# Value products joined in pairs, lower weight halves from PE, 14 raw buffers, and a refitted order

## The chip, the cores and the metric

The kernel runs on one core of one Trainium2 chip. Its engines are PE (matrix products, results in PSUM), DVE (vectors), ACT (activations and copies), POOL (general elementwise work in SBUF) and SP, whose queue issues all transfers. The metric is the device time of one launch in microseconds. PE's clock has two levels, 1.2 and 2.4 GHz; the profile shows the level that was granted as 0.50 or 1.00, and means between them.

## What is computed

Attention that keeps the 32 largest scores of each row, then a gated layer, then a layer with a softmax weighting and a normalization. The weights come as float64 words.

```python
def _attn_ref(q, k, v):            # batch 4, heads 8, rows 576, width 64
    scores = scale * np.matmul(q, k.transpose(0, 1, 3, 2))
    kth = np.partition(scores, -top_k, axis=-1)[..., -top_k:-top_k + 1]      # top_k = 32
    scores = np.where(scores >= kth, scores, -1000000000.0)
    attn = np.exp(scores - np.max(scores, axis=-1, keepdims=True))
    return np.matmul(attn / (np.sum(attn, axis=-1, keepdims=True) + 1e-09), v)

def _moe_ref(x, w_gate, w_val, w_out):          # 2304 x 512, hidden 1536
    gate = 1.0 / (1.0 + np.exp(-(x @ w_gate)))
    return gate * (x @ w_val) @ w_out

def _moe2_ref(x, w_in, w_out, g_ln):            # hidden 1024
    h = x @ w_in
    e = np.exp(h - np.max(h, axis=-1, keepdims=True))
    solu = h * e / (np.sum(e, axis=-1, keepdims=True) + 1e-09)
    ln = (solu - mean(solu)) / np.sqrt(var(solu) + 1e-06) * g_ln
    return ln @ w_out
```

## The kernel before

**Tiles.** The 2,304 rows are cut into 18 chunks of 128. A chunk has four attention steps of two heads each, 72 steps in all. In a step PE makes the scores (`scores`, L645), ACT takes them out of PSUM, DVE folds them (L656, L660) and finds the 32 largest in four rounds (L670, L674), ACT masks and exponentiates, and ACT and POOL split the result into two float16 halves (L732, L736). The queue on SP transposes both halves into a tile `et` (`flip_halves`, L743; two buffers), and PE multiplies them with the values (`attend`, L758): 30 matmuls of 64 columns of weights and 128 moving columns, two column halves of the array side by side. At the last step of a chunk PE spreads the inverse sums over the columns (`spread`, L723, also 64 columns wide), ACT copies them out (L785), and DVE scales the rows by them (L788). Then come the layers of the chunk, all products of float16 halves in three terms: gate and value (`group`, L894), down (L940), hidden (L977), last (L1088).

**Weights.** Five weights are read in 52 pieces of 128 x 512 words: gate 12, value 12, down 12, input 8, output 8, in this order. The first 36 pieces land in eight raw buffers that lie in the space of the last two weights, piece n behind piece n-8; the others land in `big`. DVE rebuilds float32 words from the two halves of each raw word (`rebuild`): two operations for the pieces in `ADDED` (the first 24), whose low bits ACT converts (`rest`, L443) and POOL adds (`add_rest`, L447); three operations for the others, the third being `low` (L433). When a weight's norm is known, a scale is formed and each piece is split: ACT writes a scaled float32 copy (`split_hi`, L501) and a float16 upper half (`split_first`, L505), and POOL subtracts (`split_lo`, L508).

**What sets the order.** Every operation is handed to a planner (`Order.add`) with an engine, a cost, a rank, its needs and the buffers that it takes and frees. The planner plays the five queues through (`play`), with a lag from each engine to each other (`SEEN`), and writes the instructions out in the order found. `SHIFT` moves ranks by kind of operation. On the chip every engine runs its instructions in that order. The first products of each weight wait for all its pieces: `done[...]` is the list of the last operations of the pieces.

Of the kernel before, what the change touches and what calls it, by code (L numbers as in the profile page):

```python
# [56 lines left out]
ADDED = tuple(range(24))  # L57
SCALED = ()
STAGED = 36
SHIFT = {  # L60
# [68 lines left out]
}  # L129
WKEYS = ("g", "v", "o1", "i", "o2")  # L130
LAYERS = ("sg", "ga", "va", "gt", "gi", "gl", "vf", "hi", "la", "th", "tl", "tf", "tu")
LONE = ("lh", "ll", "lr", "do", "n2", "p2", "s2", "mh", "mf", "ml", "l0", "l1", "l2", "l3", "ld", "l4", "fi", "sd")

# [1105 lines left out]
```

## Time and profile before

| | |
|---|---|
| median of three runs | 992.6 us (990.73 to 993.14) |
| profiled execution, its own time | 992.24 us |
| its span | 990.5 us |
| PE busy | 872.0 us (88%) |
| DVE busy | 841.0 us (85%) |
| ACT busy | 750.4 us (76%) |
| POOL busy | 617.4 us (62%) |
| 16 DMA engines, mean busy share | 45.2% on the queue of the transfers |

Busy time is the time in which an engine has an instruction under way; matmuls overlap, and their ends are modelled. In a timeline the distance between the starts of two neighbours tells what the first one cost PE, while the length printed for it contains the overlap. A row of a group of instructions gives the line, the engine, the operation, target and source, the count, then the total busy time, the mean of one in ns, and the idle time ahead of them. The span has three parts: a front in which the weights are rebuilt and the first attention steps run, a long middle, and the layers of the last chunks.

### The profile page before, as it was taken

The page shows a single profiled execution, that of the slowest core. Times are in us where ns is not written, and L with a number is a line of the kernel's source. Part 1 is how long each engine was busy: PE and PEld are TensorE (multiplying, and loading weights), DVE is VectorE, ACT ScalarE, POOL GpSimd, SP SyncE. Part 2 cuts the span into 40 slices and gives each one's busy share as a digit, 9 for nine tenths or more (in the row PEclk, how much of TensorE's full clock was granted, in tenths as well). Part 3 has the DMA queues.
Part 4 walks back from the last instruction along what each step waited for, and adds up shares of the span by engine and source line. Part 5 has one row for each costly group of instructions (what it writes and reads, how often), then busy time and mean ns, then how long its engine had stood idle before and what let it go on. Part 6 is the DMA issues. An engine that isn't in the chain of part 4 may idle for free. (4 is left out here: it accounts for less than half of the span.)

```text
span 990.5 us, 30262 instructions
## 1 busy us (share of the span) xinstructions
PE 872.0 (88%) x12244; PEld 714.2 (72%) x12244; DVE 841.0 (85%) x2234; ACT 750.4 (76%) x1433; POOL 617.4 (62%) x808
## 2 busy tenths in 40 slices
PE   2235478899999999999999999999999999999994
PEld 1114377589897978878787878797978787887962
DVE  7899999999989997999998999856799999962242
ACT  4898998988789867788899687675798787863231
POOL 7988787685877555486868564674676565551100
PEclk9997679799999999999999999999999999999997
DMA  9884646254564433265625552364625434431100
GB/s 367 319 248 111 160 144 148 55 97 114 130 156 79 106 84 68 71 140 138 142 58 110 100 93 66 88 142 118 114 48 111 95 88 84 76 84 34 24 20 13
DMA packets 231196, 109.96 MB, mean 111 GB/s; under 512 B 205712, under 2 KB 215952, under 8 KB 231056
## 3 DMA queue, kind: packets, MB, share of 16 engines
q1 hardware_dynamic: 231056, 108.03, 45.2%
q8 instruction: 96, 1.57, 0.7%
q14 instruction: 44, 0.36, 0.1%
HBM read 52.43 MB, written 4.72 MB: 58 GB/s over the span
## 5 line engine op out<-in xcount | busy, mean ns | idle before, releaser
L670 DVE MAX8 m<-w 128x8 f32<-128x288 f32 (+1 forms) x576 | 327.5, 597 | 0.6
L736 POOL TENSOR_TENSOR h<-s,h 128x576 f16<-128x576 f32 x144 | 184.6, 1287 | 103.7 <-ACT h L732 101.1
L674 DVE MATCH_REPLACE8 w<-m,w 128x288 f32<-128x288 f32 (+1 forms) x432 | 231.8, 542 | 0.0
L940 PE MATMUL px<-gh,wo 128*128 128x128 f16 x2592 | 176.4, 219 | 1.5 <-POOL gh L928 1.5
L894 PE MATMUL pg<-xt,wg 128*128 128x128 f16 x2592 | 174.3, 221 | 3.3 <-POOL xt L798 1.8
L894 PE MATMUL pv<-xt,wv 128*128 128x128 f16 x2592 | 172.6, 220 | 0.0
L940 PEld LDWEIGHTS <-wo 128*128 128x128 f16 x2592 | 151.3, 98 | 13.7 <-issue 1.9
L894 PEld LDWEIGHTS <-wv 128*128 128x128 f16 x2592 | 152.8, 98 | 10.6
L894 PEld LDWEIGHTS <-wg 128*128 128x128 f16 x2592 | 153.6, 99 | 6.7 <-issue 3.8
L645 PE MATMUL ps<-ks,qs 128*128 128x288 f32 x640 | 132.7, 335 | 27.5 <-ACT s L651 12.2
L691 ACT ACTIVATE s<-s,nk 128x576 f32<-128x576 f32 x144 | 105.5, 768 | 46.5 <-POOL nk L679 46.3
L645 PEld LDWEIGHTS ps<-ks,qs 128*128 128x128 f32 x640 | 98.5, 200 | 54.1 <-ACT s L651 20.1
L651 ACT ACTIVATE s<-ps 128x576 f32<-128x576 f32 x144 | 92.0, 639 | 38.4 <-PE ps L645 30.4
L977 PE MATMUL ph<-wi,x 128*128 128x512 f16 x432 | 120.2, 391 | 0.0
L1088 PE MATMUL po<-wo,lt 128*128 128x512 f16 x432 | 120.1, 392 | 0.0
L700 ACT ACTIVATE s<-s,nb 128x576 f32<-128x576 f32 x144 | 110.0, 765 | 0.2
L732 ACT ACTIVATE h<-s 128x576 f16<-128x576 f32 x144 | 96.0, 673 | 1.0 <-DMA lt<-lh 0.9
L758 PE MATMUL av<-et,v 128*64 128x128 f16 (+1 forms) x2400 | 79.6, 221 | 7.7 <-DMA et<-h 4.5
L758 PEld LDWEIGHTS <-v 128*64 128x64 f16 x2400 | 67.8, 114 | 22.1 <-issue 15.2
L656 DVE TENSOR_TENSOR w<-ps,s 128x576 f32<-128x576 f32 x72 | 53.9, 749 | 32.7 <-ACT s L651 16.4
L603 POOL TENSOR_TENSOR qs<-qr,qs 128x256 fp32r<-128x256 f32 x80 | 58.5, 735 | 22.5 <-ACT qs L599 22.3
L1088 PEld LDWEIGHTS <-lt 128*128 128x128 f16 x432 | 38.9, 98 | 42.4 <-issue 2.5
(171 smaller groups left out, 1317.9 us busy)
## 6 DMA issues: line engine op xcount, KB each, us to landing
kr<-in_k_dup_dram SPq DMA_DIRECT2D x32, 288.0 KB, 3.1
qr<-in_q_main_dram SPq DMA_DIRECT2D x64, 128.0 KB, 2.8
v<-in_v_pad_dram SPq DMA_DIRECT2D x16, 320.0 KB, 4.1
wi<-in_w_gate_dram SPq DMA_DIRECT2D x8, 512.0 KB, 7.1
wo<-in_w_val_dram SPq DMA_DIRECT2D x8, 512.0 KB, 8.6
wi<-in_w_out_dram SPq DMA_DIRECT2D x8, 512.0 KB, 4.4
raw<-in_w_in_dram SPq DMA_DIRECT2D x8, 512.0 KB, 4.6
raw<-in_w_out_dram SPq DMA_DIRECT2D x8, 512.0 KB, 3.3
```

The source lines that it names most:

```text
L645: nc.tensor.matmul(ps[:, t, :S // 2], q, kv["k", b, p, t][:, keys], start=y == 0, stop=y == len(mm) - 1)
L670: nc.vector.max(st["m8"][:, t, r * 8:r * 8 + 8], ranked(i, r, t))
L674: nc.vector.match_replace(w, steps[i]["m8"][:, t, r * 8:r * 8 + 8], w, LOW)
L691: nc.scalar.activation(w, w, AF.Prelu, bias=st["nk"][:, t:t + 1], alpha=PICK)
L700: nc.scalar.activation(w, w, AF.Exp, bias=st["nb"][:, t:t + 1], scale=D ** -0.5, accum_out=ch["sm"][:, y:y + 1])
L732: nc.scalar.activation(st["h"][:, 0, t], st["s"][:, t], AF.Copy)
L736: nc.gpsimd.tensor_sub(st["h"][:, 1, t], st["s"][:, t], st["h"][:, 0, t])
L758: nc.tensor.matmul(ch["av"][j * D:(j + 1) * D, p, st["o"]:st["o"] + wd], v, e[:, y * REM:y * REM + wd], start=one and k == (0, 5)[j], stop ...
L894: nc.tensor.matmul(dst, w[a][:, c, f * P:(f + 1) * P], ch["xt"][:, b, c], start=x == 0, stop=x == len(mm) - 1)
L940: nc.tensor.matmul(ch["px"][:, e], wo1h[a][:, f, e * P:(e + 1) * P], ch["gh"][:, b, f], start=y == 0, stop=y == len(DOWN) - 1)
L977: nc.tensor.matmul(ch["ph", nn], ch["x2"][:, a, c], wih[b][:, c, nn * 512:(nn + 1) * 512], start=c == 0 and a == 0 and b == 0, stop=c == K ...
L1088: nc.tensor.matmul(ch["po"], ch["lt"][:, a, f], wo2h[b][:, f], start=y == 0, stop=y == len(FIN) - 1)
```

## The change

- `attend` now runs for two steps at a time: one operation of the planner multiplies the values of steps i-1 and i, and at the last step of a chunk the spreading product stands in front of them in the same operation. It needs both transposes and frees both `et` buffers at its end. The copy of the spread rows now comes behind the whole run.
- For the first 36 pieces (`BYPE`: gate, value, down) the lower half comes from PE. A diagonal matrix with the weight's scale is formed once for each weight; PE multiplies the float32 piece by it into a PSUM buffer (`pm`, four of them, shared with the rebuilding and the layers), the float16 upper half is written as before by ACT or, for every second piece (`HIPOOL`), by POOL, PE adds the upper half times minus one, and ACT copies the rest out as float16.
- All 52 pieces are in `ADDED`: two operations on DVE, one on ACT, one on POOL.
- The raw buffers are 14 for the first 14 pieces (six more, in the space of the down weight), then eight as before.
- The first products of a weight wait for the pieces that they read, not for the whole weight.
- The planner adds 0.6 us to every lag into PE from another engine, from the fourth chunk or the thirteenth step on, and 1.2 us to each load of a piece. The shifts are fitted anew.
- The spreading product uses minus the identity, and the row factors change their sign with it. The trace of the norms is written over its PSUM source, and there are five buffers of the eight-largest lists in place of six.

```diff
-ADDED = tuple(range(24))
+ADDED = tuple(range(52))
 SCALED = ()
+BYPE = tuple(range(36))
+HIPOOL = tuple(range(0, 36, 2))
 STAGED = 36
...
+SLACK = 600
+STEPWISE = ("qd", "qb", "qa", "qk", "se", "fm", "fn", "m", "r", "nk", "nb", "be", "ex", "hh", "hl", "tr", "at")
...
+    def extra(self, name, engine, other):
+
+        if name[0] == "wd":
+            return 2 * SLACK
+        if engine != "PE" or other == "PE" or len(name) < 2 or not isinstance(name[1], int):
+            return 0
+        return SLACK if name[1] >= (12 if name[0] in STEPWISE else 3) else 0
...
+        ahead = [([], op[5], [(t, seen[op[0]][taker[t]] + op[8] + self.extra(name, self.TAKER[t], self.ENGINES[op[0]])) for t in op[6]])
+                 for name, op in zip(names, ops)]
...
-                lag = seen[ops[y][0]][op[0]] + ops[y][8]
+                lag = seen[ops[y][0]][op[0]] + ops[y][8] + self.extra(names[x], self.ENGINES[op[0]], self.ENGINES[ops[y][0]])
...
-    ident16 = cp.tile([P, P], F16, name="ident16")
-    nc.vector.tensor_copy(ident16, ident)
+    minus16 = cp.tile([P, P], F16, name="minus16")
+    nc.vector.tensor_scalar(minus16, ident, -1.0, None, op0=OP.mult)
+    diag = cp.tile([P, P], F32, name="diag")
...
+    def slot(n):
+        return n if n < 14 else (n - 14) % 8
+
+    def readers(x, n):
+
+        last = [y for y in range(min(n, STAGED)) if slot(y) == x][-1:]
+        return [(k, *pieces[y]) for y in last for k in ("wr", "wz") if (k, *pieces[y]) in order.ops]
...
-                raw = (wi[:, n % 4] if n % 8 < 4 else wo2[:, 2 * (n % 4):2 * (n % 4) + 2].rearrange("p a b -> p (a b)")).bitcast(U64)
+                x = slot(n)
+                raw = wi[:, x] if x < 4 else (wo2 if x < 8 else wo1)[:, 2 * (x % 4 if x < 8 else x - 8):][:, :2].rearrange("p a b -> p (a b)")
+                raw = raw.bitcast(U64)
...
-            junk = tl(sp, [P, P], BF16, "jk", "jk", 1)
-            nc.vector.scalar_tensor_tensor(junk, state["q", x][:, 0], 1.0, ident, op0=OP.mult, op1=OP.mult,
+            nc.vector.scalar_tensor_tensor(state["q", x][:, 0], state["q", x][:, 0], 1.0, ident, op0=OP.mult, op1=OP.mult,
...
+        def diagonal():
+            nc.vector.tensor_scalar(diag, ident, scale[key][0], None, op0=OP.mult)
+
+        def scaled_pe(f, c):
+            state["pw", f, c] = pw = tl(pp, [P, 512], F32, "pw", "pm")
+            nc.tensor.matmul(pw, diag, piece(f, c), start=True, stop=False)
+
+        def first_pe(f, c):
+            if number[f, c] in HIPOOL:
+                nc.gpsimd.tensor_scalar(hi_[:, c, f:f + 512], piece(f, c), scale[key][0], 1.0, op0=OP.mult, op1=OP.mult)
+            else:
+                nc.scalar.activation(hi_[:, c, f:f + 512], piece(f, c), AF.Copy, scale=scale[key][0])
+
+        def minus_pe(f, c):
+            nc.tensor.matmul(state["pw", f, c], minus16, hi_[:, c, f:f + 512], start=False, stop=True)
+
+        def rest_pe(f, c):
+            nc.scalar.activation(lo_[:, c, f:f + 512], state["pw", f, c], AF.Copy)
+
...
-            add(("wd", *W), "DMA", 1.46, t - 8, lambda f=f, c=c: fetch(f, c), [x for x in (("wr", *pieces[n - 8]), ("wz", *pieces[n - 8])) if x in order.ops] if staged and n >= 8 else [],
+            add(("wd", *W), "DMA", 1.28, t - 8, lambda f=f, c=c: fetch(f, c), readers(slot(n), n) if staged else [],
                 take=[] if staged else ["big"], delay=0.95, room=None if staged else lambda f=f, c=c: room(f, c))
-            after = [x for y in pieces[STAGED - 8:STAGED] for x in (("wr", *y), ("wz", *y)) if x in order.ops] if key in ("i", "o2") else []
+            after = readers(dict(o1=8 + c // 2, i=c, o2=4 + c // 2)[key], n) if key in ("o1", "i", "o2") else []
...
+        if any(number[y] in BYPE for y in todo):
+            add(("wdg", key), "DVE", 0.2, t, diagonal, [("wc", key)] + [name for name in order.ops if name[0] == "we"])
         for x, (f, c) in enumerate(todo):
             W = (key, f, c)
+            if number[f, c] in BYPE:
+                add(("we", *W), "PE", 0.9, t + 0.6 * x, lambda f=f, c=c: scaled_pe(f, c), [("wdg", key)], take=["pm"])
+                add(("wh", *W), *(("POOL", 0.68) if number[f, c] in HIPOOL else ("ACT", 0.75)), t + 0.6 * x, lambda f=f, c=c: first_pe(f, c), [("we", *W)])
+                add(("wf", *W), "PE", 0.25, t + 0.6 * x, lambda f=f, c=c: minus_pe(f, c), [("wh", *W)])
+                add(("wl", *W), "ACT", 0.62, t + 0.6 * x, lambda f=f, c=c: rest_pe(f, c), [("wf", *W)], free=["pm"])
+                continue
             pool = number[f, c] in SCALED
...
-        return [("wl", key, f, c) for f, c in todo]
+        return {(f, c): ("wl", key, f, c) for f, c in todo}
...
-            st["m8"] = sp.tile([P, 2, TOPK], F32, name=f"m8{i}", tag="m8", bufs=6)
+            st["m8"] = sp.tile([P, 2, TOPK], F32, name=f"m8{i}", tag="m8", bufs=5)
...
-                                         ident16[:, rows], start=a == 0, stop=a == 1)
+                                         minus16[:, rows], start=a == 0, stop=a == 1)
...
     def attend(i):
+        if steps[i]["last"]:
+            spread(steps[i]["ch"])
+        attend_one(i - 1)
+        attend_one(i)
+
+    def attend_one(i):
...
-        nc.vector.tensor_scalar(f, scale[key][0], scale[f"x{b}"][1], 1.0 / PROB, op0=OP.mult, op1=OP.mult)
+        nc.vector.tensor_scalar(f, scale[key][0], scale[f"x{b}"][1], -1.0 / PROB, op0=OP.mult, op1=OP.mult)
...
-        needs = [("tr", i)] + [("vl", b, p, x) for p in st["pairs"] for x in range(2)]
-        needs += [("at", i - 1)] * (i > 0 and not st["first"])
-        add(("at", i), "PE", 1.18 if rem else 1.06, e + 6, lambda i=i: attend(i), needs,
-            take=["av"] if st["first"] else [],
-            free=["et"] + ["v"] * sum(uses[b, p][-1] == i for p in st["pairs"]))
+        if i % 2:
+            pair = (steps[i - 1], st)
+            needs = [("tr", i - 1), ("tr", i)] + [("vl", y["b"], p, x) for y in pair for p in y["pairs"] for x in range(2)]
+            needs += [("at", i - 2)] * (not pair[0]["first"])
+            if st["last"]:
+                needs += [("ih", ch["x"])] + [("va", ch["x"] - 1, 7)] * (ch["x"] > 0)
+            add(("at", i), "PE", (2.17 if rem else 1.93) + 0.27 * st["last"], e + 6, lambda i=i: attend(i), needs,
+                take=["av"] * pair[0]["first"] + ["pm"] * st["last"],
+                free=["et"] * 2 + ["v"] * sum(uses[steps[y]["b"], p][-1] == y for y in (i - 1, i) for p in steps[y]["pairs"]))
...
-            add(("rb", x), "PE", 0.46, e + 5, lambda ch=ch: spread(ch), [("ih", x)] + ([("va", x - 1, 7)] if x else []), take=["pm"])
-            add(("rs", x), "ACT", 0.5 if len(ch["vs"]) == 1 else 0.7, e + 5, lambda ch=ch: take_spread(ch), needs[1:] + [("rb", x)], take=["xf"], free=["pm"])
+            add(("rs", x), "ACT", 0.5 if len(ch["vs"]) == 1 else 0.7, e + 5, lambda ch=ch: take_spread(ch), needs, take=["xf"], free=["pm"])
...
-               [("xl", x)] + done["g"] * (x == 0) + [("ga", x, f - 1)] * (f % 4 > 0) + [("do", x - 1, 0)] * (f % 4 == 0 and x > 0),
+               [("xl", x)] + [done["g"][f // 4 * 512, c] for c in range(KD)] * (x == 0) + [("ga", x, f - 1)] * (f % 4 > 0) + [("do", x - 1, 0)] * (f % 4 == 0 and x > 0),
...
-            needs += [[("gl", x, 8)] + done["o1"] * (x == 0), [("gi", x, 0), ("gi", x, 4)], [("gl", x, 0), ("gl", x, 4)]][y % 3]
+            needs += [[("gl", x, 8)], [("gi", x, 0), ("gi", x, 4)], [("gl", x, 0), ("gl", x, 4)]][y % 3]
+            needs += [done["o1"][0, c] for c in (range(8, 12) if y % 3 == 0 else range(8))] * (x == 0)
...
-            needs = needs + [("la", x, y - 1)] * (y > 0) + done["o2"] * (x == 0)
+            needs = needs + [("la", x, y - 1)] * (y > 0) + [done["o2"][0, c] for c in range(KF2) if c <= (3 * y + 2) // 2] * (x == 0)
```

## Rows read from the trace of the kernel before

**Rows 1.** Busy us of each engine in four stretches, with granted clock and DMA share.
```profile
core 0: us, PE busy (x) PEld busy (x) DVE busy (x) ACT busy (x) POOL busy (x), PEclk, DMA share, GB/s
0.00:28.80 28.80, 8.16 (x55) 6.50 (x56) 22.60 (x43) 13.42 (x20) 21.77 (x23) 1.00 0.95 372
28.80:131.30 102.50, 39.94 (x284) 28.96 (x283) 98.41 (x234) 97.00 (x173) 85.71 (x91) 0.81 0.67 199
131.30:200.00 68.70, 57.33 (x786) 49.71 (x784) 66.83 (x181) 62.22 (x113) 49.14 (x58) 0.89 0.42 107
200.00:913.00 713.00, 701.53 (x10406) 581.97 (x10406) 630.76 (x1719) 556.46 (x1090) 454.63 (x628) 1.00 0.46 98
```

**Rows 2.** Timeline of PE: start us, length us, line, products, count; around one value run.
```profile
369.89 0.83 PE L894 MATMUL pg<-xt,wg 128*128 128x128 f16 x12
370.56 0.83 PE L940 MATMUL px<-gh,wo 128*128 128x128 f16 x12
371.33 1.03 PE L758 MATMUL av<-et,v 128*64 128x128 f16 x30
372.29 0.84 PE L940 MATMUL px<-gh,wo 128*128 128x128 f16 x12
```

**Rows 3.** Timeline of PE where value runs and the spreading product touch or stand alone.
```profile
222.90 0.64 PE L723 MATMUL rb<-ident,ih 128*64 128x128 f16 x16
223.47 0.84 PE L940 MATMUL px<-gh,wo 128*128 128x128 f16 x12
...
534.00 1.03 PE L758 MATMUL av<-et,v 128*64 128x128 f16 x30
534.86 0.61 PE L723 MATMUL rb<-ident,ih 128*64 128x128 f16 x16
535.31 1.00 PE L758 MATMUL av<-et,v 128*64 128x128 f16 x30
536.24 0.85 PE L977 MATMUL ph<-wi,x 128*128 128x512 f16 x3
```

**Rows 4.** The transposes: SP's waits (us, times, longest), landing, one step, value products after 200.
```profile
SPq L743 <- PE av L758: 24.9, 11, 4.2
...
DMA to landing us min/median/max: 3.9/4.1/7.4
...
458.68 1.86 SPq L743 DMA_TRANSPOSE et<-h  x1
...
472.34 1.03 PE L758 MATMUL av<-et,v 128*64 128x128 f16 x30
...
L758 PE MATMUL av<-et,v 128*64 128x128 f16 (+1 forms) x2130 | 66.3, 215 | 2.5 <-DVE xf L788 1.5 <-POOL v L635 0.9
```

**Rows 5.** Groups of instructions on ACT and POOL that the weights' edits resemble.
```profile
L505 ACT ACTIVATE wg<-wg,sc_g 128x512 f16<-128x512 f32 x12 | 10.2, 857 | 0.0
L785 ACT ACTIVATE xf<-rb 128x512 f32<-128x512 f32 x16 | 9.4, 587 | 3.8 <-PE rb L723 3.7
L501 ACT ACTIVATE ts<-wg,sc_g 128x512 f32<-128x512 f32 x12 | 8.4, 711 | 0.7 <-POOL wg L508 0.4 <-POOL wv L447 0.3
L443 ACT ACTIVATE rs<-wi 128x512 int32<-128x512 uint32 x12 | 8.0, 664 | 5.1 <-DMA wi<-in_w_gate_dram 3.0 <-POOL wg L447 2.1
...
L508 POOL TENSOR_TENSOR wv<-ts,wv 128x512 f16<-128x512 f32 x12 | 15.1, 1279 | 0.1
L1044 POOL TENSOR_SCALAR e<-e,st 128x1024 f32<-128x1024 f32 x16 | 19.3, 1207 | 1.7
```

**Rows 6.** PE: first gate product, float32 products between others, and a group of float32 records.
```profile
131.30 3.09 PE L894 MATMUL pg<-xt,wg 128*128 128x128 f16 x36
...
953.55 0.66 PE L1062 MATMUL pl<-ident,e 128*128 128x128 f32 x4
954.04 0.83 PE L940 MATMUL px<-gh,wo 128*128 128x128 f16 x12
...
L388 PE MATMUL ptot<-r,ones 128*128 128x1 f32 x18 | 3.4, 258 | 4.4 <-DVE r L478 4.4
```

**Rows 7.** The third operation of a rebuilt piece on DVE.
```profile
L433 DVE SCALAR_TENSOR_TENSOR wo<-wi,pd 128x512 uint32<-128x512 uint32 x8 | 5.4, 672 | 0.0
```

More of the change, by code (lines that the diff above doesn't have):

```diff
@@ L198, in seq, with links @@
             needs, take = [(*name, "part", x)], ()
-    def run(self):
+    def extra(self, name, engine, other):
[4 more added lines that the diff above has]
+        return SLACK if name[1] >= (12 if name[0] in STEPWISE else 3) else 0
+    def links(self):
         num = {e: x for x, e in enumerate(self.ENGINES)}
@@ L205, in run @@
         taker = {t: num[e] for t, e in self.TAKER.items()}
-        ahead, back = ([([], op[5], [(t, seen[op[0]][taker[t]] + op[8]) for t in op[6]]) for op in ops],
-                       [([], op[6], [(t, self.BACK) for t in op[5]]) for op in ops])
+        names = list(self.ops)
+        ahead = [([], op[5], [(t, seen[op[0]][taker[t]] + op[8] + self.extra(name, self.TAKER[t], self.ENGINES[op[0]])) for t in op[6]])
+                 for name, op in zip(names, ops)]
+        back = [([], op[6], [(t, self.BACK) for t in op[5]]) for op in ops]
         for x, op in enumerate(ops):
             for y in (place[n] for n in op[4]):
-                lag = seen[ops[y][0]][op[0]] + ops[y][8]
+                lag = seen[ops[y][0]][op[0]] + ops[y][8] + self.extra(names[x], self.ENGINES[op[0]], self.ENGINES[ops[y][0]])
                 ahead[y][0].append((x, lag))
                 back[x][0].append((y, lag))
-        self.ends, order, self.end = self.play(ops, ahead, [op[2] for op in ops], True)
+        return ops, ahead, back
+    def run(self):
+        ops, ahead, back = self.links()
+        place = {name: x for x, name in enumerate(self.ops)}
+        best = [op[2] for op in ops]
+        self.ends, order, self.end = self.play(ops, ahead, best, True)
         assert order, "no order"
@@ L220, in run @@
                 break
-            ends, found, end = self.play(ops, ahead, [total - t for t in ends], True)
+            rank = [total - t for t in ends]
+            ends, found, end = self.play(ops, ahead, rank, True)
             if not found:
@@ L224, in run @@
             if end < self.end:
-                order, self.end, self.ends = found, end, ends
+                order, self.end, self.ends, best = found, end, ends, rank
+        if MOVED:
+            for name, by in MOVED.items():
+                best[place[name]] += round(by * 1000)
+            self.ends, order, self.end = self.play(ops, ahead, best, True)
+            assert order, "no order"
         last, items, names = [0] * 5, [], list(self.ops)
@@ L526, in weights @@
             if by_column:
-                add(("wq", *W), "ACT", 0.52, t, lambda f=f, c=c: square(f, c), [("wx" if added else "wr", *W)], take=["x2"])
+                add(("wq", *W), "ACT", 0.52, t, lambda f=f, c=c: square(f, c), [("wx" if added else "wr", *W)] + [("wq", key, *todo[x - 1])] * (x > 0), take=["x2"])
                 add(("wp", *W), "PE", 0.22, t, lambda f=f, c=c: columns(f, c),
@@ L779, in row_factors @@
             yield (slice(x * n, x * n + n),
-                   1.0 / PROB if own else factors["row", ch["key"], b])
+                   -1.0 / PROB if own else factors["row", ch["key"], b])
     def take_spread(ch):
@@ L806, in body @@
         for j in range(2):
-            add(("kd", b, p, j), "DMA", 0.85, t - 3 * STEP, lambda b=b, p=p, j=j: load_k(b, p, j),
+            add(("kd", b, p, j), "DMA", 1.0, t - 3 * STEP, lambda b=b, p=p, j=j: load_k(b, p, j),
                 ([("qk", uses[b - 1, p][-1], 1)] if b else []) + [("kd", b, p, 0)] * j, take=["big"], delay=0.95)
@@ L812, in body @@
                 [("kb", b, p, j)], free=["big"])
-        add(("vd", b, p), "DMA", 0.91, t - STEP, lambda b=b, p=p: load_v(b, p), take=["v"], delay=0.95)
+        add(("vd", b, p), "DMA", 1.1, t - STEP, lambda b=b, p=p: load_v(b, p), take=["v"], delay=0.95)
         add(("vn", b, p), "ACT", 0.75, t + STEP, lambda b=b, p=p: norm_v(b, p), [("vd", b, p)], take=["xf"], free=["xf"])
@@ L1117, in body @@
             op(("ga", f), "PE", 0.687, f, lambda ch=ch, f=f: gate(ch, f),
-               [("xl", x)] + done["g"] * (x == 0) + [("ga", x, f - 1)] * (f % 4 > 0) + [("do", x - 1, 0)] * (f % 4 == 0 and x > 0),
+               [("xl", x)] + [done["g"][f // 4 * 512, c] for c in range(KD)] * (x == 0) + [("ga", x, f - 1)] * (f % 4 > 0) + [("do", x - 1, 0)] * (f % 4 == 0 and x > 0),
                take=["pm"] if f % 4 == 0 else [])
         for y, f in enumerate((8, 0, 4)):
-            op(("sg", f), "ACT", 0.58, 12, lambda ch=ch, f=f: squash(ch, f), [("ga", x, f + 3), ("fs", key)] + done["v"] * (x == 0),
+            op(("sg", f), "ACT", 0.58, 12, lambda ch=ch, f=f: squash(ch, f), [("ga", x, f + 3), ("fs", key)] + [("wx" if ("we", *n[1:]) in order.ops and ("wx", *n[1:]) in order.ops else "wl", *n[1:]) for n in done["v"].values()] * (x == 0),
                take=["two"], free=["pm"])
@@ L1124, in body @@
             op(("va", f), "PE", 0.687, 12 + y + (y > 9), lambda ch=ch, f=f: value(ch, f),
-               [("xl", x)] + done["v"] * (x == 0) + [("va", x, f - 1)] * (f % 4 > 0) + [("ga", x, f + 3)] * (f % 4 == 0) +
+               [("xl", x)] + [done["v"][f // 4 * 512, c] for c in range(KD)] * (x == 0) + [("va", x, f - 1)] * (f % 4 > 0) + [("ga", x, f + 3)] * (f % 4 == 0) +
                [("va", x, 3), ("va", x, 11)] * (f == 7),
@@ L1150, in body @@
         for y in range(8):
-            needs = [("mh", x)] + [("tu", x - 1, 1) if x - 1 in LATE else ("lr", x - 1)] * (x > 0 and y == 0) + done["i"] * (x == 0) + [("hi", x, y - 1)] * (y > 0) + [("ml", x)] * (y >= 5)
+            needs = [("mh", x)] + [("tu", x - 1, 1) if x - 1 in LATE else ("lr", x - 1)] * (x > 0 and y == 0) + [done["i"][y // 2 * 512, c] for c in range(KD) if x == 0 and y in (0, 2)] + [("hi", x, y - 1)] * (y > 0) + [("ml", x)] * (y >= 5)
             op(("hi", y), "PE", 0.677, 47 + y, lambda ch=ch, y=y: hidden(ch, y), needs, take=["pm"] if y in (0, 2) else [],
```

8 lines of the change are left out of this document (5 added, 3 removed), and 148 rows, old and new, of the table SHIFT.

## The prediction

> **What bounds the kernel now.** The profiled execution took 992.24 us, 1.7 us more than its span of 990.5; the three timed runs have their median at 992.6, 0.4 above it. I make the sum on the span, add 1.7, and let the 0.4 be.
>
> I read the table of windows first [rows 1]. From 200 to 913 us PE is busy 701.5 of 713 us, at a granted clock of 1.00, so it stands still for 11.5 us only. DVE stands still for 82 us in the same stretch, ACT for 157. PE bounds this part, and every microsecond of work taken from PE there comes off the end, as long as DVE keeps up. Before that PE is nearly idle. Up to 131.3 us, where the first gate product starts, it is busy 48.1 of 131.3, while DVE is busy 121.0 and ACT 110.4. From 28.8 us on, when the first weight's total stands, DVE is busy 98.4 and ACT 97.0 of 102.5 us. So the front is bound by DVE and ACT together: attention steps and the rebuilding and splitting of weights share them. From 131.3 to 200 PE still has 11.4 us of gaps. The chain of the last chunk at the end is left as it is by the change.
>
> One page speaks against this reading. The Trainium skill (Perfetto Trace Analysis, Identifying the Most-Contended Engine) doesn't let PE be judged by its matmul time but by its weight loads, and then takes the busiest engine as the bound. By it DVE (631 us from 200 to 913) would stand before PE's loads (582 us), and the change would be worth its DVE time alone; that is the second rival below. The gaps speak against it: DVE waits for 82 us there, PE for 11.5.
>
> **Value products in pairs.** A run of 64-column matmuls costs something at each end. Twelve 128-column matmuls take 0.67 us from start to start (369.89 to 370.56), the twelve ahead of a value run take 0.77: 0.10 to go in. The run itself takes 0.96 before another form (371.33 to 372.29) [rows 2] but 0.86 where the spreading product follows it (534.00 to 534.86) [rows 3]: 0.10 to come out. Two steps apart cost 2 x 1.06 = 2.12, joined 0.10 + 0.86 + 0.96 = 1.92. The spreading product takes 0.57 alone (222.90 to 223.47) and 0.45 with value products behind it [rows 3]; with its way in that is 0.67 against 0.45. There are 36 pairs and 18 spreads: 36 x 0.20 + 18 x 0.22 = 11.2 us, less about 1 us for those that already touch by chance, as the one in rows 3 does. About 9 of the 10 lie after 200 us, where PE is the bound: **-9 us**. Bounds: -6 (half of them already touch) and -11. The copy of the spread rows, so far ahead of the last value products, now comes behind them; for the first chunk its 0.59 us [rows 5] lies on the path to the first gate product, and I let the front's term below hold it.
>
> The join also holds both transposed tiles (two buffers) until the second step's products are done. The queue that issues the transposes stands behind that buffer: it already waited 24.9 us, 11 times, for value products [rows 4]. This is the third rival below. I count nothing for it in the sum, because a pair comes every two steps, some 22 us (2,130 of the 2,400 value products, so 64 of 72 steps, run in the 713 us), and its two transposes of some 2 us, 4.1 us to landing and 1.9 us of products fill about 10 [rows 4].
>
> **Lower halves by PE, for 36 pieces.** Taken away: a scaled copy on ACT (0.711), and a subtraction on POOL (1.279) [rows 5]. Put in: a float32 matmul against a diagonal, a float16 one that takes the upper half off, and an ACT copy out of PSUM; half of the upper halves go from ACT (0.857) to POOL.
> - ACT: -36 x 0.711 = -25.6 and -18 x 0.857 = -15.4. The copy out of PSUM lies between 0.587 (float32 to float32, no gaps between elements) and 0.857 (float16 written at every second place) [rows 5]; I take 0.74, halfway, for it has the one's source and the other's target: 36 x 0.74 = +26.6 (21 to 31). Together -14.4 (-20 to -10).
> - POOL: -36 x 1.279 = -46.0. The scaling of 512 elements costs between 0.60 (half of the scaling of 1024, 1.207) and 1.28 (a subtraction of the same size) [rows 5]; I take 0.68, a little above the half of its own kind: +12.2 (11 to 23). Together -34.
> - PE: a float32 product shows two records for each call (18 for nine calls), and four float32 passes of 128 columns took 0.49 us where matmuls run at full clock (953.55 to 954.04) [rows 6], so 512 columns in two records are about 2 x 0.49 = 0.98 us; the float16 one is 4 x 128 columns, a third of 0.67 = 0.22 [rows 2]. That is 1.2 us a piece and 43 us for 36; at the half clock 2.4 and 86. The lower bound is a single record, 0.7 a piece and 25 us.
>
> The gate's and the value's 24 pieces lie ahead of 131.3 us (the first gate product, [rows 6]), where PE has 102.5 - 39.9 = 62.6 us free after 28.8 [rows 1]: 29 us at 2.4 GHz, 58 at 1.2 GHz. Both fit, so I count nothing; without that cover it is the fourth rival. The twelve of the down projection come around and after the start of the layers: 12 x 1.2 = 14.4, of which the 11.4 us of gaps hold most: **+3 us** (0 to +14). The waits between the four steps of a piece are covered by other pieces, four PSUM buffers being there; DVE's rebuilding shares them.
>
> **The last 28 pieces are added on POOL.** Taken away: 28 x 0.672 = 18.8 us of DVE [rows 7]. Put in: 28 x 0.664 = 18.6 us on ACT, and an addition on POOL that I price as the subtraction: 28 x 1.279 = 35.8 [rows 5]. With the part before: DVE -18.8 (+0.6 for three diagonals, by the nearest of DVE's small operations some 0.2 each), ACT +4.2 (-1 to +9), POOL +2 (+1 to +13).
>
> So DVE gives up 18 us, while ACT, which works beside it, gets 4 more. Of the 171.2 us from 28.8 to 200, ACT is busy 159.2 [rows 1]; with 4.2 more, some 8 are left, and the front can hardly be shorter by more than that unless ACT starts earlier. It is idle for 15 of the first 28.8 us, and the 14 raw buffers in place of 8 could fill some of that; but the DMA engines are busy at 0.95 there already [rows 1], so loads can come little earlier. Waits for single pieces instead of whole layers let products start some pieces sooner. I take **-5 us** for the front, between 0 (ACT holds it) and -18 (DVE's whole relief).
>
> **More lag into PE.** The planner now holds PE's work 0.6 us behind its inputs. This can only remove short waits: all of the gaps from 200 to 913 are 11.5 us [rows 1]. I take **-3** (0 to -8). One buffer fewer for the eight largest, the sign moved into the row factors, the trace written in place: no operation more, counted at nothing; the fifth of these buffers is still four steps behind.
>
> **Sum:** -9 + 3 - 5 - 3 = -14; 990.5 - 14 + 1.7 = **978 us**, with 970 to 986 as this case's own range.
>
> **The rivals.**
> 1. *Only the joins pay.* ACT holds the front as now, no gap of PE goes: -9 + 3 = -6, so 986 (983 to 991). For it: ACT at 97.0 of 102.5 us. Against it: ACT idle at the start.
> 2. *DVE's relief comes through whole*, because the new order moves ACT's work to the first 30 us: -9 + 3 - 18 - 3 = -27, so 965 (958 to 970). By the rule of the Trainium skill above (Perfetto Trace Analysis), with DVE as the only bound, it would be -18 alone, 974. For it: DVE's 121.0 of 131.3 us. Against it: ACT.
> 3. *The pair holds the transposes* (slower). A step's products run long after their transpose: issued at 458.68, multiplied at 472.34, 13.7 us later [rows 4]. If a pair stands like that, the next transpose, ready a step (713 / 64 = 11.1 us) after the last, waits 13.7 + 1.9 - 11.1 = 4.5 us, and with it the buffer that DVE needs for its next step. DVE's 82 idle us cover 18 such stops of the 32 pairs after 200 us. From there each costs 4.5: at 21 pairs +13. DVE is the bound then, so joins and lag give nothing, and the front's 5 come off: 1000 (993 to 1010). Against it: the queue's longest stop for value products is 4.2 us now [rows 4], and DVE has three such buffers.
> 4. *The half clock in the front.* The granted clock is 0.81 from 28.8 to 131.3 [rows 1], and all 36 pieces at 1.2 GHz ahead of the first gate product are 86 us for 62.6 free: the layers start 23 us later, 9 + 3 come off, so 1004. The Trainium skill (TensorE: Matmul & The Clock Gate, What's actually happening) holds the throttled state to be the default that activity releases. By that rule denser products would raise the clock and undo this case. No row here shows so dense a front.
> 5. That the change doesn't do what it says has little room: the operations are written out. What it can fail at is the order, which is rivals 1, 3 and 4.
>
> **How the numbers follow.** Forecast 0.40; only joins 0.20; whole relief 0.16; held transposes 0.14; half clock 0.10. What a measurement of this kernel tells from no change is about 0.3%, 3 us around 992.6. Faster: 0.40 + 0.16 + 0.15 of the joins = 0.71. Same: 0.05 of the joins and 0.03 of the held transposes = 0.08. Slower: 0.21. The range goes from 960, which leaves the lowest part of the whole relief out (0.04), to 995, which leaves most of rivals 3 and 4 out (about 0.16).
>
> **What would show it.** The joins: value runs of 60 matmuls with the spreading product in front, 36 runs in place of up to 90, and PE's work after 200 us less by 9. The front: the first gate product at about 126 us rather than 131.3, with ACT without gaps ahead of it. The diagonal products: about 1 us each at the full clock. The lag: PE's gaps from 200 to 913 under 9 us. The forecast is wrong if the first gate product starts later than 131.3 (rival 4), if it starts before 116 (rival 2), or if DVE waits for transposes in the middle (rival 3).

## The result, and the profile after

The changed kernel takes 976.65 us (976.29 to 976.97) against 992.87 for the kernel before: a ratio of 0.984, interval 0.9823 to 0.9857, 16.2 us less. The forecast was 978 with 960 to 995. Its profiled execution has a span of 974.7 us, 15.8 under the 990.5 of before. The size is the forecast's; its terms were not, as the rest shows.

First the table of windows after, with the columns of [rows 1]: us, busy time and instructions of PE, of its weight loads, DVE, ACT and POOL, then PE's granted clock, the DMA share and GB/s.

```profile
0.00:28.80 28.80, 7.11 (x42) 5.68 (x42) 17.39 (x38) 15.92 (x28) 20.22 (x22) 1.00 0.93 349
28.80:131.30 102.50, 66.31 (x354) 35.68 (x355) 100.19 (x243) 92.92 (x172) 83.04 (x95) 0.90 0.62 197
131.30:200.00 68.70, 67.58 (x1025) 58.30 (x1025) 68.06 (x175) 67.61 (x124) 58.67 (x70) 1.00 0.56 140
200.00:913.00 713.00, 699.19 (x10477) 586.87 (x10476) 623.53 (x1709) 558.21 (x1092) 458.85 (x627) 1.00 0.45 97
```

Against [rows 1]: from 131.3 to 200 us PE is full, 67.6 of 68.7 us where it was busy 57.3. From 200 to 913 its gaps have not shrunk, they are 13.8 us after 11.5.

The same windows for PE alone say where the 15.8 us are. They need only one cut, at 200 us. Before:

```profile
0.00:200.00 200.00, 105.43 (x1122) 0.86 0.62 192
200.00:913.00 713.00, 701.53 (x10406) 1.00 0.46 98
913.00:1005.00 92.00, 65.01 (x720) 0.93 0.06 18
```

After:

```profile
0.00:200.00 200.00, 141.00 (x1419) 0.95 0.65 199
200.00:913.00 713.00, 699.19 (x10477) 1.00 0.45 97
913.00:1005.00 92.00, 49.27 (x460) 0.93 0.04 13
```

A span is 200 us, plus PE's work behind them, plus what PE stands still behind them. Before: 200 + 766.5 + 24.0. After: 200 + 748.5 + 26.2. So PE's work behind 200 us is 18.0 less, and its idle time 2.2 more. Part of the 18.0 is work that the joins took away, part is work that was done ahead of 200 us. PE's groups by line, up to 200 us (line, tiles, count, then busy us and mean ns), show the latter:

```profile
L980 PE MATMUL pg<-xt,wg 128*128 128x128 f16 x288 | 19.3, 219 | 0.0
L980 PE MATMUL pv<-xt,wv 128*128 128x128 f16 x264 | 16.4, 219 | 0.0
L841 PE MATMUL av<-et,v 128*64 128x128 f16 x300 | 10.9, 238 | 0.0
L1026 PE MATMUL px<-gh,wo 128*128 128x128 f16 x144 | 9.4, 219 | 0.4 <-POOL gh L1014 0.4
```

Before, 228 gate, 144 value, 270 attention and 144 down products were done by then, though the first gate product comes later now, at 145.56 us where it came at 131.30 [rows 6].

The joined runs, in PE's timeline (start, length, line, products, count):

```profile
369.28 0.83 PE L980 MATMUL pv<-xt,wv 128*128 128x128 f16 x12
370.05 1.87 PE L841 MATMUL av<-et,v 128*64 128x128 f16 x60
371.84 0.85 PE L1026 MATMUL px<-gh,wo 128*128 128x128 f16 x12
...
209.29 0.64 PE L800 MATMUL rb<-minus,ih 128*64 128x128 f16 x16
209.76 1.84 PE L841 MATMUL av<-et,v 128*64 128x128 f16 x60
```

A pair takes 1.79 us from start to start, 0.77 ahead of it, and the spreading product in front 0.47. These are close to the forecast's prices (1.82, 0.77, 0.45). PE's timeline has 36 separate value runs, 31 of them behind 200 us; before it had 85, 75 of them behind 200 us.

The edits on the weights, as groups (busy us, mean ns, idle ahead):

```profile
L841 PE MATMUL av<-et,v 128*64 128x128 f16 (+1 forms) x2400 | 70.3, 219 | 0.0
L565 PE MATMUL pw<-wo,diag 128*128 128x512 f32 x24 | 12.0, 612 | 0.0
L574 PE MATMUL pw<-wo,minus 128*128 128x512 f16 x12 | 4.4, 390 | 1.4 <-POOL wo L569 1.1 <-ACT wo L571 0.2
L577 ACT ACTIVATE wg<-pw 128x512 f16<-128x512 f32 x12 | 8.5, 746 | 1.1 <-PE pw L574 1.1
L571 ACT ACTIVATE wv<-wv,sc_v 128x512 f16<-128x512 f32 x6 | 5.2, 862 | 0.0
L569 POOL TENSOR_SCALAR wv<-wv,sc_v 128x512 f16<-128x512 f32 x6 | 5.1, 864 | 2.9 <-PE pw L565 2.9
```

### The profile page after: what moved, and what is told of

The parts are those of the page before. It is cut to its first block, busy times and chain, and to the rows that moved or that the text cites. A ratio compares the mean times of both kernels' runs of the same rounds, so it can differ in the third digit from the quotient of the medians.

```text
span 974.7 us, 30501 instructions
## 1 busy us (share of the span) xinstructions
PE 889.5 (91%) x12351; PEld 718.5 (74%) x12352; DVE 827.8 (85%) x2209; ACT 750.7 (77%) x1443; POOL 622.6 (64%) x818
## 5 line engine op out<-in xcount | busy, mean ns | idle before, releaser
L980 PE MATMUL pg<-xt,wg 128*128 128x128 f16 x2592 | 169.8, 219 | 1.9 <-POOL xt L881 1.0
L980 PE MATMUL pv<-xt,wv 128*128 128x128 f16 x2592 | 170.6, 219 | 0.9 <-ACT sg L1003 0.9
L980 PEld LDWEIGHTS <-wg 128*128 128x128 f16 x2592 | 151.1, 98 | 7.1 <-issue 2.1
L722 PE MATMUL ps<-ks,qs 128*128 128x288 f32 x640 | 130.2, 330 | 20.9 <-POOL ks L692 7.9
L722 PEld LDWEIGHTS ps<-ks,qs 128*128 128x128 f32 x640 | 95.7, 195 | 42.1 <-ACT s L728 13.2
L1063 PE MATMUL ph<-wi,x 128*128 128x512 f16 x432 | 117.8, 388 | 1.3 <-issue 1.3
L733 DVE TENSOR_TENSOR w<-ps,s 128x576 f32<-128x576 f32 x72 | 54.1, 752 | 29.1 <-PE ps L722 10.8
L841 PE MATMUL av<-et,v 128*64 128x128 f16 (+1 forms) x2400 | 70.3, 219 | 0.0
L1063 PEld LDWEIGHTS <-x 128*128 128x128 f16 x432 | 37.7, 97 | 43.7 <-issue 1.5
L841 PEld LDWEIGHTS <-v 128*64 128x64 f16 x2400 | 65.5, 114 | 4.3 <-issue 2.9
```

What stands on the lines that cost most here:

```text
L722: nc.tensor.matmul(ps[:, t, :S // 2], q, kv["k", b, p, t][:, keys], start=y == 0, stop=y == len(mm) - 1)
L841: nc.tensor.matmul(ch["av"][j * D:(j + 1) * D, p, st["o"]:st["o"] + wd], v, e[:, y * REM:y * REM + wd], start=one and k == (0, 5)[j], stop ...
L980: nc.tensor.matmul(dst, w[a][:, c, f * P:(f + 1) * P], ch["xt"][:, b, c], start=x == 0, stop=x == len(mm) - 1)
L1063: nc.tensor.matmul(ch["ph", nn], ch["x2"][:, a, c], wih[b][:, c, nn * 512:(nn + 1) * 512], start=c == 0 and a == 0 and b == 0, stop=c == K ...
```

## The experiments

The theory: the front is bound by DVE and ACT together, PE's new work hides there, and behind 200 us PE's work is the bound. The rivals: DVE alone bounds (its relief whole), the joined pair holds the transposes, the half clock makes the new products long. In the first four kernels every engine keeps the order of the changed kernel (but for the products that e_split moves), and the edit sits inside single operations.

**e_split: the joined runs cut open.** In 44 of 54 seams a 128-column product that came later anyway is moved in between two value runs, or behind the spreading product. In outline, not in the code's words:

```diff
-    spread; attend_one(i - 1); attend_one(i)
+    spread; <next ready 128-column run>; attend_one(i - 1); <next>; attend_one(i)
```

> The changed kernel with its order kept, but the joined runs cut open again at 44 of their 54 seams: between the spreading product, the first step's and the second step's value products, 128-column products that followed in PE's order anyway are moved in. No work is added; only the changes of form come back. Theory (PE is the bound from the first gate product on, and a change into and out of a 64-column run costs 0.20 us): 44 x 0.20 = +9 us, 985 to 987. Rival (DVE is the bound, by the rule of the Trainium skill's Perfetto Trace Analysis that judges PE by its weight loads): within 2 us of the changed kernel's 976.7.

Measured: 981.16 us (979.71 to 981.48), 4.5 more than the changed kernel. PE's windows:

```profile
200.00:913.00 713.00, 704.10 (x10403) 1.00 0.44 96
913.00:1005.00 92.00, 52.88 (x533) 0.96 0.05 15
```

PE's work behind 200 us is 757.0, so 8.5 more. All 44 seams lie there (75 separate value runs behind 200 us, as in the kernel before, for 31), so it is 0.19 us a seam, near the forecast's 0.20. The idle time behind 200 us fell from 26.2 to 22.3: PE reached its waits later and waited less. So 4.0 of the joins' 8.5 us never reached the end, and the time lies between what the theory (985 to 987) and the rival (within 2 us of 976.7) had expected.

**e_short: the float32 product against the diagonal is left out**, a bf16 one stands in its place.

```diff
-            nc.tensor.matmul(pw, diag, piece(f, c), start=True, stop=False)
+            upper = dst.bitcast(BF16).rearrange("p k (n w) -> p k n w", w=2)[:, c, f:f + 512, 1]
+            nc.tensor.matmul(pw, upper[:, :P], upper, start=True, stop=False)
```

> The changed kernel with its order kept; it leaves out the float32 product with the diagonal for the 36 pieces and puts a bfloat16 product of 512 columns in its place, so PE has about 36 x 0.65 = 23 us less to do in the front. Theory (that work lies in PE's idle time): -3 to 0 us, 974 to 977, with the first gate product still near 145 us. Rival (the added work holds the front back, as the late first gate product suggests): -10 us or more, 967 or less, with the first gate product near 130.

Measured: 976.76 us (975.81 to 977.74), no change. PE from 28.8 to 131.3 us, with the columns of [rows 1]:

```profile
28.80:131.30 102.50, 57.04 (x326) 30.51 (x327) 99.90 (x242) 92.63 (x171) 83.35 (x96) 0.74 0.65 195
```

PE has 9.3 us less work there (11.7 up to 200 us), the first gate product starts at 145.56 us as in the changed kernel, and the end does not move: what the float32 products cost beyond bfloat16 ones is hidden, as the forecast counted them. The other products of the 36 pieces stayed in, so for them it is not shown. The granted clock is 0.74 in place of 0.90, which the last section takes up.

**e_dve: the last 28 pieces repeat a DVE operation.** DVE's busy time rises by 18.1 us (827.8 to 845.8), about what the operation that the change took out had cost (28 of 0.672 us, [rows 7]).

```diff
-                return [(0.6, first), (0.6, lambda: top(piece(f, c).bitcast(U32)))]
+                def both():
+                    top(piece(f, c).bitcast(U32))
+                    if number[f, c] >= 24:
+                        top(piece(f, c).bitcast(U32))
+                return [(0.6, first), (0.6, both)]
```

> The changed kernel with its order kept; for the last 28 pieces DVE repeats its second operation, so that the 18.8 us that the change takes from DVE are put back, and nothing else. Theory (DVE and ACT bound the front together; DVE has about 5 us to spare ahead of 200 us): +10 to +15 us, 987 to 992. Rival 1 (ACT alone holds the front): 0 to +4, 977 to 981. Rival 2 (DVE's relief came through whole): +18 or more, 995.

Measured: 994.14 us (992.85 to 996.74), 17.5 more. PE up to 200 us:

```profile
0.00:200.00 200.00, 130.92 (x1158) 0.91 0.61 190
```

261 products fewer than the changed kernel's 1,419 are done by then; PE's work behind 200 us is 763.9, 15.4 more. The time lies between the theory's 987 to 992 and the 995 of the rival in which DVE's relief counts whole, nearer the rival.

**e_act: the lower halves are copied out twice.** ACT's busy time rises by 26.5 us (750.7 to 777.2). The second copy also holds its PSUM buffer longer, which this run does not separate.

```diff
-            nc.scalar.activation(lo_[:, c, f:f + 512], state["pw", f, c], AF.Copy)
+            for _ in range(2):
+                nc.scalar.activation(lo_[:, c, f:f + 512], state["pw", f, c], AF.Copy)
```

> The changed kernel with its order kept; ACT copies each of the 36 lower halves out of PSUM twice, 36 x 0.745 = 26.8 us more on ACT, about what the scaled copies cost that the change takes away (25.6). Theory (ACT bounds the front beside DVE): +12 to +22 us, 989 to 999. Rival (DVE alone is the bound and ACT has room): 0 to +5, 977 to 982.

Measured: 1003.04 us (1002.12 to 1004.68), 26.4 more.

```profile
0.00:200.00 200.00, 123.66 (x993) 0.91 0.59 186
```

PE's work behind 200 us is 775.0, 26.5 more, the whole addition, and more than the 12 to 22 us expected. So with the order kept, time added to DVE and time added to ACT both count, in full or nearly, and neither is alone the bound. The other engines then wait: from 131.3 to 200 us DVE and ACT were both full in the changed kernel (68.1 and 67.6 of 68.7 us); e_dve and e_act in the same stretch, with the columns of [rows 1]:

```profile
131.30:200.00 68.70, 60.87 (x787) 47.61 (x786) 68.18 (x166) 63.49 (x115) 50.67 (x59) 1.00 0.52 130
```

```profile
131.30:200.00 68.70, 55.79 (x704) 40.67 (x703) 54.46 (x134) 68.09 (x119) 41.41 (x53) 0.98 0.47 119
```

What PE can't do by 200 us it does at the end.

**Single parts, with the order fitted again.** A part left out needs another order. For the next eight kernels I fitted `SHIFT` anew by random steps on the planner's own end, starting from the changed kernel's shifts, or from those of before where its code is the base.

*f_nojoin*: the changed kernel without joins.

```diff
-        if i % 2:
-            pair = (steps[i - 1], st)
...
+        add(("at", i), "PE", 1.18 if rem else 1.06, e + 6, lambda i=i: attend(i), needs,
```

> The changed kernel without the joins (one run of value products for each step, the spreading product by itself), all else of the change kept and the order fitted anew for it. With the order kept, cutting 44 seams cost 4.5 us of the 9 that the changes of form make up; the rest went into gaps of PE. Theory (joins are worth about half to three quarters of their 10 us, since PE has gaps of 14 us between 200 and 913): +5 to +8, 982 to 985. Rival (they are worth the whole sum, as predicted): +9 to +11, 986 to 988.

Measured: 992.2 us (991.37 to 994.86), 15.5 more than the changed kernel and above both expectations. *f_join*: the kernel before with the joins alone (the same lines the other way).

> The kernel before with the joins alone (pairs of steps, spreading product in front), no lower half by PE, eight raw buffers, no added lag, order fitted anew for it. Theory (half to three quarters of 10 us): -5 to -8 against the kernel before, 984 to 988. Rival (whole sum): -9 to -11, 981 to 983. If the held transposes matter, it is not below 990.

Measured: 988.27 us (986.6 to 989.61), ratio to before 0.9947 (0.993 to 0.9964). PE's work behind 200 us is 758.3, 8.2 under before; its idle time 29.4, 5.4 over. The gain of 4.5 falls just short of the 5 to 8 expected.

*f_add24*: the third DVE operation is back for the last 28 pieces (`ADDED = tuple(range(24))`).

> The changed kernel with the third operation on DVE put back for the last 28 pieces in place of ACT's conversion and POOL's addition (DVE +18.8, ACT -18.6, POOL -35.8), order fitted anew for it. With the order kept, 18.8 us more on DVE alone cost 17.5, and 26.8 more on ACT cost 26.4. Theory (both engines are one chain in the front, so that what one gives the other takes): within 5 us of the changed kernel, 977 to 982. Rival (DVE is the bound, its relief counts alone): +12 to +18, 989 to 995.

Measured: 991.95 us (989.21 to 994.23), in the rival's range. *f_noby*: ACT and POOL make all lower halves (`BYPE = ()`, `HIPOOL = ()`).

> The changed kernel with the lower halves made as before for all pieces (scaled copy on ACT, subtraction on POOL, no product on PE): PE -41, ACT +14.4, POOL +31, order fitted anew for it. Theory (ACT's time in the front counts in full, PE's not at all): +12 to +18, 989 to 995. Rival (the lower halves by PE are worth nothing by themselves, since PE's share costs what ACT's gives): within 4 us, 973 to 981.

Measured: 996.3 us (994.53 to 998.21), just above the theory's. *f_slack0*: no added lag (`SLACK = 0`).

> The changed kernel with the added lag set to zero (no 0.6 us into PE, no 1.2 us per load) and the order fitted anew for that by an annealing of the shifts. Theory of the forecast (the lag takes short waits of PE away, worth 3 us): PE's gaps from 200 to 913 us grow from 13.8 to some 17, and the time is 977 + 3 = 980. Rival, from the changed kernel's trace, where the gaps are 13.8 in place of 11.5 though the lag is there: the lag is worth nothing, or costs what it holds back; the gaps stay within 1 us of 13.8 and the time is 974 to 978. A second fit of an order is itself a handicap of some us against the first one, so a result up to 980 speaks for neither.

Measured: 991.77 us (990.17 to 994.33); PE's gaps from 200 to 913 us are 20.2; neither expectation had so much. *f_lag*: the kernel before with the lag alone.

> The kernel before with the added lag alone, the order fitted anew for it. Theory of the forecast: PE's gaps from 200 to 913 us fall from 11.5 to under 9 and the time is 993 - 3 = 990. Rival: the gaps do not fall, and operations held back behind their inputs make the front longer: the first gate product comes later than 131.3 us and the time is 995 or more.

Measured: 1001.36 us (1000.96 to 1002.83); PE's gaps there 12.6, so they did not fall. The time is the rival's, but not its sign: the first gate product comes earlier, at 123.12 us.

Five of these six stand at 988 to 996, whichever part is missing or stands alone. That asks what a second fit does by itself. *f_ctrl* is the changed kernel whole, fitted again from the shifts of before; *f_cost* is it whole, fitted again with three costs set to the durations in the trace.

> The control for the runs with a second fit: the changed kernel with every part of it, its order fitted anew by the same annealing, from the shifts of the kernel before. Nothing of the work is different. If a second fit costs nothing, the time is that of the changed kernel, 977 within 2, and the 15 us that the runs without joins, without POOL's share and without lag stood above it belong to those parts. If the second fit is itself the handicap, the time is 985 to 993, with PE's idle time near 95 us in place of 85, and those runs bound the worth of their parts from above only, by their difference to this one.

> The changed kernel with three of the planner's costs set to what the trace shows: POOL's upper half 0.86 in place of 0.68 us, ACT's upper half 0.86 in place of 0.75, ACT's copy out of PSUM 0.74 in place of 0.62; the order fitted anew for them. Theory: the planner's front was too fast by 36 x 0.12 + 18 x 0.11 = 6 us on ACT and 18 x 0.18 = 3 us on POOL, so the plan and the chip drift apart there, and an order fitted to the measured durations is up to 5 us faster than the control with the planner's own costs. Rival: such small errors do not matter, since every engine keeps its order and the time is given by the work: within 3 us of the control.

Measured: f_ctrl 974.67 us (972.65 to 979.19), ratio to before 0.9823 (0.9801 to 0.9844); f_cost 990.04 us (988.13 to 991.32), ratio 0.9965 (0.9954 to 0.9977). PE's windows of f_ctrl, from an execution of 979.2 us, the longest of its own:

```profile
0.00:200.00 200.00, 150.57 (x1508) 0.91 0.63 200
200.00:913.00 713.00, 690.12 (x10355) 1.00 0.45 96
913.00:1005.00 92.00, 51.94 (x493) 0.93 0.05 15
```

and of f_cost:

```profile
0.00:200.00 200.00, 136.30 (x1254) 0.91 0.62 195
200.00:913.00 713.00, 699.05 (x10430) 1.00 0.45 97
913.00:1005.00 92.00, 62.45 (x673) 0.93 0.06 18
```

The same work in three orders takes 975, 977 and 990 us. f_ctrl came near the 977 that was expected if a second fit costs nothing, f_cost near the 985 to 993 if it is itself the handicap. Both expectations for f_cost fell: better prices made the order neither faster nor equal. So the six kernels ahead of these don't price their parts: whether 15 us are a missing part or another order can't be told from them. Where a fit starts may count too: f_nojoin, f_add24, f_noby, f_slack0 and f_cost started from the changed kernel's shifts, f_ctrl from those of before. Against f_cost those four are 2 to 6 us slower, against f_ctrl 17 to 22; a control from the changed kernel's shifts at its own costs was not run. What all of them do show is the account of PE's work behind 200 us and its idle time there (us, from each kernel's windows):

| kernel | products by 200 us | work behind | idle behind | span |
|---|---|---|---|---|
| before | 1,122 | 766.5 | 24.0 | 990.5 |
| after | 1,419 | 748.5 | 26.2 | 974.7 |
| e_short | 1,381 | 747.9 | 26.6 | 974.4 |
| f_ctrl | 1,508 | 742.1 | 35.3 | 977.4 |
| e_split | 1,422 | 757.0 | 22.3 | 979.3 |
| f_join | 1,116 | 758.3 | 29.4 | 987.7 |
| f_cost | 1,254 | 761.5 | 26.4 | 987.9 |
| f_nojoin | 1,373 | 763.3 | 27.3 | 990.6 |
| f_slack0 | 1,310 | 756.9 | 33.7 | 990.6 |
| f_add24 | 1,103 | 766.0 | 25.8 | 991.8 |
| e_dve | 1,158 | 763.9 | 29.1 | 993.0 |
| f_noby | 1,005 | 767.4 | 27.0 | 994.4 |
| f_lag | 1,032 | 774.5 | 25.0 | 999.5 |
| e_act | 993 | 775.0 | 26.1 | 1001.1 |

Of the products by 200 us, 108 are those of the 36 pieces (72 in e_short; none in before, f_join, f_noby and f_lag). The work behind 200 us moves by 33 us over the table, the idle time by 13, and most of the order of the spans is the work's; f_slack0 is the exception, with e_split's work and 11.4 us more of idle time. f_ctrl is as fast as the changed kernel or a little faster (their intervals overlap): a version beside it, not one shown to beat it.

## Why the prediction was right, point by point

- **PE is the bound behind 200 us, the front is DVE's and ACT's.** Right for the second half: e_dve and e_act both cost in full or nearly. For the first, "every microsecond of work taken from PE there comes off the end" failed: e_split gave back 8.5 us of PE's work and lost 4.5 us of time. PE at 98% still waits, and with less work it arrives at a wait earlier.
- **The joins, -9.** The mechanism and the price were right: 0.19 us a seam where the forecast's 11.2 us over 54 seams are 0.21; the value products' own busy time fell from 79.6 to 70.3 us. As a term of the sum it was twice too large: 4.5 us with the order kept. f_join's 4.5 under before agrees, but lies within what an order alone can move.
- **Lower halves by PE, nothing and +3.** The nothing was right (e_short). The products were busy for longer than priced: 14.3, 12.2 and 12.0 us for three weights and 13.7 for taking off the upper halves, 52 in all for 43. The +3 is not seen: the last product of the 36 pieces starts at 146.2 us and 10.7 us of their work lies behind 131.3 us, where PE has hardly a gap, but e_short has 65.1 us of work from 131.3 to 200 in place of 67.6 and the end does not move. What the products that stayed in cost there is not shown. ACT's copy out of PSUM took 0.738 to 0.748 us for the 0.74 taken. POOL's upper half took 0.843 to 0.864 for 0.68, a quarter more, 3 us over 18 pieces.
- **The front, -5.** This is the term that carried the result. Of the 18.0 us of work that left PE's part behind 200 us, 8.5 are the joins' by e_split, whose separate value runs behind 200 us are as many as before, so 9.5 were done earlier, for the forecast's -5 + 3 = -2. That is a difference, not a run of its own, but the counts of products agree: behind 200 us the changed kernel has 180 gate and value products fewer, 10 us at 0.67 for twelve, and the other groups together take about 1 off that (an estimate from counts and starts). DVE's busy time fell by 13.2 us in place of 18 (841.0 to 827.8), ACT's rose by 0.3 in place of 4 (750.4 to 750.7). e_dve and e_act show that time added to either costs nearly its whole in this order; what taking it away gave, in an order fitted to it, they do not show. Which part of the edit brought the 9.5 (the added pieces, the products on PE, the buffers, the finer waits, the new order) stays open.
- **The first gate product at 126.** Failed: it starts at 145.56, where the text had named a start after 131.3 as the sign of rival 4. Yet the time is the forecast's. The marker was wrong: f_ctrl starts it at 112.73 us and f_cost at 124.35, and their times are 15 us apart; f_lag, the slowest of the new fits, starts it at 123.12. Here are PE's products around it:

```profile
143.53 1.87 PE L841 MATMUL av<-et,v 128*64 128x128 f16 x60
145.33 0.40 PE L574 MATMUL pw<-wo,minus 128*128 128x512 f16 x1
145.56 0.83 PE L980 MATMUL pg<-xt,wg 128*128 128x128 f16 x12
```

PE had multiplied the values of six attention steps by then (four at the start of before's first gate product) and all products of the 36 pieces but the last subtraction, and it is hardly idle, 1.1 us from 131.3 to 200. What is left at a fixed time is the measure, not when one kind of work begins.
- **The lag, -3.** As forecast it failed: the gaps from 200 to 913 us went from 11.5 to 13.8, not under 9, and the idle time behind 200 us from 24.0 to 26.2. But e_split has 8.9 us of gaps there and 22.3 of idle time: without the joins' saving the rest of the change has less idle time than the kernel before, by 1.7 us. Whether that is the lag's is not shown: f_lag (12.6) has no fewer gaps for it, and f_slack0 has 20.2 without the lag, but f_ctrl 22.9 with it.
- **Rival 2, DVE's relief whole (965).** Its time did not come. ACT was as tight, as the row of ACT said, but e_dve's 17.5 us and f_add24's 15.3 lie nearer to this rival than to the forecast's share for DVE; f_add24 can't be told from a worse order. The Trainium skill's rule (Perfetto Trace Analysis, Identifying the Most-Contended Engine), which ranks the busiest engine without PE's matmul time, would have named DVE (623.5 us from 200 to 913 against 586.9 of PE's loads). The traces agree only in part: DVE's added time counts nearly whole in e_dve, ACT's counts too in e_act, though ACT's 750.7 us are less than DVE's 827.8.
- **Rival 3, the transposes held.** The stops of the queue came; its slowdown did not. SP's wait for value products (us, times, longest) and DVE's step operation from 200 to 913 us with what it waited for:

```profile
SPq L820 <- PE av L841: 97.3, 20, 17.2
...
L733 DVE TENSOR_TENSOR w<-ps,s 128x576 f32<-128x576 f32 x59 | 44.4, 753 | 27.3 <-PE ps L722 10.8 <-ACT s L728 7.6 <-DMA lt<-lh 3.1
```

The queue stood 97.3 us in place of 24.9 [rows 4], up to 17.2 at once, where the rival had worked with stops of 4.5. f_join has 93.3 too, f_nojoin 32.8, so it is the joins. DVE hardly felt it: ahead of that operation it waits 3.1 us for a transfer of the last layer (2.9 before) and 0.7 for a transpose of `et`, and its idle time from 200 to 913 rose only from 82 to 89.5. ACT did wait for the transposes of `et`, 11.7 us in six waits (2.7 in one before, 3.9 in two in f_join). Whether that reached the end no run separates: e_split still holds both transposes of a pair.
- **Rival 4, the half clock.** Did not come: the clock from 28.8 to 131.3 us rose from 0.81 to 0.90. That denser products would undo this rival fits the rows; see below.

So the sum of -14 met -15.8 by errors of opposite sign, and that the number came so close is luck. In the account of work and idle time the forecast was -9 for the joins, -2 for front and pieces, -3 of idle time; measured were -8.5, -9.5 and +2.2. The front was 7.5 too small, the idle time 5.2 too good. What the joins lose on their way to the end (4.0 of 8.5) stands in that idle time. Counted by what reached the end, with e_split, the joins are -4.5, the front and pieces -9.5, the other idle time -1.7.

## What to carry to other kernels

Work taken away from an engine that is 98% busy need not come off the end whole (here 4.5 of 8.5 us): the engine waits where it did not before, and a run in the kept order tells how much. Measure a front by the bound engine's work that is left at a fixed time, not by when the next stage starts. And where a planner fits the order, fit the whole change again, from the same start, before pricing its parts by leaving one out: here the same work took 975 to 990 us in three orders, about as much as the change gained.

## What the runs showed of the hardware

**Denser products went with a higher clock.** PE from 100 to 131.3 us (us, busy and count, granted clock, DMA share, GB/s), before:

```profile
100.00:131.30 31.30, 14.12 (x134) 0.59 0.64 166
```

and e_short, then the changed kernel, with the columns of [rows 1]:

```profile
100.00:131.30 31.30, 20.50 (x147) 11.48 (x147) 30.53 (x85) 30.16 (x56) 22.89 (x30) 0.76 0.53 128
```

```profile
100.00:131.30 31.30, 26.02 (x165) 13.96 (x165) 30.90 (x87) 30.49 (x56) 22.44 (x29) 1.00 0.52 129
```

With 14.1, 20.5 and 26.0 us of work in the same stretch the clock was 0.59, 0.76 and 1.00. With the float32 products the stretch was granted full speed throughout, with bfloat16 ones in their place it was not; whether their length or their type counts is not separated. The Trainium skill (TensorE: Matmul & The Clock Gate, What's actually happening) says that the throttled state is the default and activity releases it; these rows agree.

**A seam of tile shapes costs 0.19 us**, in and out together (8.5 us for 44 in e_split). The Trainium skill (TensorEngine Tiling (Array Packing), Key Properties) says that a change of the tiling mode drains the engine, and gives no price. The rows agree that a change costs time and give a price; that the engine drains no row shows.

**POOL's scaling took longer into float16 at every second place.** From float32 to float32 it took 1,207 ns for 1,024 elements [rows 5], by half of that an estimated 0.60 us for 512; to float16 at every second place 0.843 to 0.864 us for 512. Type, spacing and length differ between the two, and no run separates them.
